# Gated mix of a segment-recurrent attention and a linear-memory attention: float32 partial rows of the output projection, a query pass in column halves, and one attention mask as a matmul

## The chip, the cores and the metric

The kernel runs on one core of a Trainium2 chip. The metric is the device time of one execution in microseconds (us), median of three runs. The engines are called as the profile calls them: PE (TensorE, with PEld for its weight loads), DVE (VectorE), ACT (ScalarE), POOL (GpSimd) and SP (SyncE, which here only issues DMAs, in order, and waits in order).

## The reference

Two attentions read the same 2048 tokens of width 512 and are mixed by a gate per token.

```
# A: 64 segments of 32 tokens, 8 memory tokens carried from one to the next
for s in range(n_seg):
    h = concatenate([mem, x[s*32:(s+1)*32]])          # 40 rows
    q, k, v = h @ Wq, h @ Wk, h @ Wv                  # 32 heads of 128
    p = softmax(where(mask, q k^T * scale, -1e9))     # memory columns open, the rest causal
    o = (p v) @ Wo
    mem = o[:8];  outs.append(o[8:])
# B: 4 blocks of 512 tokens, 32 heads of 16: causal softmax in the block,
#    plus phi(q) M / phi(q) z with M, z summed over the blocks before
g = sigmoid((x * gate_w).sum(-1))
out = g * a + (1 - g) * b
```

The memory of a segment is the first 8 rows of the output of the one before. So the 64 segments of A form one chain, while B and everything that does not depend on the memory can run beside it.

## The kernel before

**How A is cut.** In segment `s` only 32 rows go through the passes that the memory gates: the 8 memory rows and the first 24 tokens. The last 8 tokens of each of four segments (a group, `g = s // 4`, 16 groups) are "left" rows: they need no memory as inputs, and their queries, keys and values are projected together for the group (units `L<g>.…`, `left_units`). The 32 heads lie in two halves, 0 and 1, of 16 heads. Each unit of work has a short name, and `A_ORDER` is a string, written out in full, in which every unit of the whole kernel stands once; `plan_a` walks it, and each unit appends its instructions to the queues of its engines (lines 1678 to 1680). Engines run their queues in order and wait on semaphores; so the string sets the order on each of PE, DVE, ACT, POOL and SP. A `~` behind a name swaps the engine of a copy out of PSUM between ACT and DVE; `A_ENG` has the default.

For segment `s` the units are:

- `K0x K0y K1x K1y Q0x … V1y`: the projections. A pass is for one of K, Q, V and one half of the heads and gives a bank of 512 columns; `x` and `y` are the first and the last two of the four blocks of the contraction (`nat_pass` L1471, `proj` L1248). Each is 8 matmuls, four beside each other in column strips of the array, 512 columns each.
- `k0 k1 q0 q1 v0 v1`: the copies out of PSUM (`nat_ev` L1477). `TK0 TK1 TQ0 TQ1`: transposes on DVE, 128x256 four-byte elements each (`tr` L1486, `flip` L1262).
- `qt`: POOL copies the left queries of the segment beside the others (L1651).
- `S0 S1`: scores on PE (L1498). `X0 X1`: exp on ACT (L1517). `Y0 Y1`: the mask, a `min` with `mkeep` on DVE (L1522; `mkeep` holds 3e38 where a score counts and 0 elsewhere). `M0 M1`: sums on PE by a matmul with ones (L1529). `L0 L1`: reciprocals as ln and exp on ACT (L1543). `N0 N1`: the product on DVE (L1551); `n0 n1`: the product for the left rows on POOL (L1555).
- `PV`: values (L1560), which needs both halves. `E0 … E3`: four copies out (L1586). `W0 … W3`: the product with Wo (L1594, `out_part` L1332): 64 matmuls in all into one bank of 128x256, in which partitions 0 to 63 hold one partial sum (over 16 heads) and 64 to 127 the other.
- `hm`: the recurrence. DVE transposes that bank (L1606), moves half of it (L1607) and adds the two partial sums into the next segment's columns of `xTp` (two instructions, L1611).
- `G` and `H`: the same bank is copied out for the output rows, its two partition halves into `WF[0]` and `WF[1]` (`half_out` L1358, twice 64x256 float32). `ws`: POOL adds them into `WN[s % 2]` in bfloat16 (`sum_rows` L1361), and SP stores that to DRAM as `aTd[s]` (`rows_out` L1365).
- `oL`: POOL keeps the attention output of the left rows in `OTL` (L1632).

For a group: `O<g>.0 … 3` is the product of `OTL` with Wo, `O<g>.e`, `.f` are its two copies, and `.s` the sum on POOL and the store to `aTl[g]` (`ol_units` L1369). `T<g>.l` loads the rows of the group into `aTg` (`load` L1408): four segments, for each a DMA of 24 rows from `aTd` (L1415) and one of 8 rows from `aTl` (L1417), eight in all, six for the last group. `T<g>.b` is B's output projection on PE, and it issues the load of B's next rows; `.t` puts `(1-g)` times it into `t1_sb` on ACT (L1446); `.f` adds `g` times `aTg` on DVE (L1458) and stores the result. The last segment's rows do not go that way: `63.H` finishes them from the bank and stores them by four DMAs.

For B: `bS` (scores of two steps), `bE` (exp on ACT, and for tiles on the diagonal a mask on POOL by `affine_select`, L945), `bP` (values), `bT` (what closes a job), `pj` and `pp` (projections of the last block). B issues its loads as it goes, on SP too, and most of them wait for PE to have read the buffer they fill.

**Before the string** come the loads of x and the weights and B's projections of three blocks; the weights Wk, Wq, Wv of A are loaded in that order.

**Waits.** `_mk_deps` (L88) makes an instruction that writes a tile wait for all readers of it, DMAs included; loads with `scratch=True` wait for the DMAs that stored their rows. DMAs are issued by SP in the string's order.

Of the kernel before, what the change touches and what calls it, by code (L numbers as in the profile page):

```python
# [238 lines left out]
def build(nc, es, A_x, A_mem0, A_Wq, A_Wk, A_Wv, A_Wo, B_wq, B_wk, B_wv, B_wo, B_beta, gate_w, out, dbg=None):  # L239
# [31 lines left out]
    def alloc(stack, *specs):  # L271
        at, spans = 0, {}
        for name, shape, dt, n in specs:
# [15 lines left out]
          ("onesb", [128, 128], BF16, 0), ("mkeep", [128, 224], BF16, 0),  # L289
# [5 lines left out]
          ("WN", [128, 256], BF16, 2), ("tt", [128, 2 * C, SEG], F32, 0), ("tu", [128, 2 * C, M], F32, 0), ("WF", [128, 256], F32, 2), ("OLN", [128, 256], BF16, 0))  # L295
# [17 lines left out]
    v.t1z = v.KTL0[:, :, :, :, :, :].rearrange("p r j k m u -> p (r j k m u)").bitcast(F32)[:, 0:128]  # L313
    v.KTL, v.QTL, v.VL = [v.KTL0, v.KTL1], [v.QTL0, v.QTL1], [v.VL0, v.VL1]
# [3 lines left out]
    def dram(name, shape):  # L318
        t = nc.dram_tensor("scr_" + name, shape, BF16, kind="Internal")
        setattr(v, name, t.ap())  # L320
# [4 lines left out]
    dram("aTd", [NSEG, 64, 256])  # L325
    dram("aTl", [NG, 64, 256])
# [98 lines left out]
def plan_const(v):  # L425
# [29 lines left out]
    def late():  # L455
        rob, rmk = Rs("onesb"), Rs("mkeep")
        gp(lambda g: g.memset(onesb[:], 0.0), rob, "onesb0", True)
# [5 lines left out]
        for j in range(4):  # L463
# [5 lines left out]
            for n in range(2):  # L469
# [5 lines left out]
        v.late_mask = lambda: P.op("dve", lambda d: d.transpose(mkeep[:, :].rearrange("p (i w) -> p i w", w=L + 16)[:, :, L:L + 16], v.mskT[:, :, :, :, :].rearrange("p n (x k) m u -> p (n x) (k m u)", x=2)),  # L475
             reads=[rmt], writes=[rmk], name="mskT")
# [377 lines left out]
class BAttn:  # L854
# [190 lines left out]
    L0.xl 0.K0x L0.QL1x L0.QL0x wl L0.VL0x L0.VL1x wl L0.QL1y L0.VL0y L0.VL1y 0.V0x 0.K0y L0.KL1x L0.VL0e~ L0.KL1y 0.K1x L0.KL0x 0.K1y L0.VL1e L0.KL0y wl  # L1045
    L0.QL0y 0.Q1x L0.KL1e~ 0.Q0x 0.k1~ wl L1.xl 0.k0 L0.KL0e~ L0.QL1e bS L0.QL0e bE 0.TK0 0.Q1y L1.KL0x wl bE bE wl 0.Q0y 0.V1x 0.V1y 0.qt pj 0.q0 0.q1
    0.TQ1 L0.VLt 0.TQ0 0.TK1 pj pj wl 0.S1 0.S0 0.V0y 0.X0 0.Y0 0.X1 pj L1.KL0y 0.Y1 0.v0 0.M1 bE 0.M0 0.L1 L1.KL0e L1.QL0x wl bP L1.QL0y 0.n1 0.L0 0.N1
    0.N0 1.qt 0.v1~ bP 0.n0 0.PV 0.E1 0.E0 0.W0 0.E3~ pp~ 0.E2 bS 0.W1 0.W2 bE 0.W3 bE pj pj bE bE bP bP 0.hm 0.G~ 1.K0x 1.K0y 1.Q0x pp 1.k0~ 1.Q0y 1.K1x
    1.q0~ L1.QL0e~ 1.K1y 1.TK0 1.TQ0 0.H 0.oL 1.Q1x 1.Q1y bS 1.k1 1.V0x pp~ 1.S0 1.q1 bE 1.V0y 1.TK1 1.X0 1.TQ1 1.S1 1.V1x 1.Y0 1.M0 1.v0 bE 1.V1y 1.X1
    1.Y1 bE 1.M1 1.L0 1.v1 pj 1.L1 1.n0 1.N0 pj 1.N1 1.n1 L1.KL1x bE 1.PV 1.E0 1.E1 L1.KL1y bP bP 1.W0 0.ws 1.E2~ 1.W1 1.E3~ 1.W2 pp L1.KL1e~ 1.W3 1.hm bS  # L1050
    1.G~ pj pj bE bE bE 2.qt 2.K1x 2.Q0x 2.Q0y bT 2.K0x 1.H 2.K1y bE 2.q0~ bP 2.K0y bS 2.k1~ pp bP bE bE bE bE 2.k0~ 2.V1x 2.Q1x 2.Q1y 1.ws 2.TK1 2.TQ0
    2.V1y 2.TK0 2.S0 L1.QL1x 2.q1~ 2.TQ1 2.V0x 2.S1 pj 2.X0 2.Y0 1.oL 2.M0 2.v1~ pj 2.X1 2.L0 2.Y1 2.M1 2.V0y bP pj 2.n0 2.N0 pp~ bP 2.L1 pj 2.v0~ 2.N1 pj
    2.n1 2.PV pj 2.E0~ L1.QL1y pp 2.E2 2.E1 2.E3~ L1.QL1e~ 2.W0 2.W1 2.W2 2.W3 bS 3.qt pp~ bE 2.hm bE bE L1.VL0x L1.VL0y 3.K1x 2.G~ 3.K0x L1.VL0e bE 3.K0y
    3.Q1x 3.k0 3.Q1y bT bP 2.H 3.K1y bS 3.TK0 3.q1 3.k1 bP 3.TQ1 3.Q0x 3.Q0y 3.V1x bE 3.TK1 3.q0 3.S1 bE 3.V1y 3.TQ0 pj 3.S0 3.V0x bE 3.X1 3.Y1 3.v1 bE
    3.X0 3.M1 3.L1 pj 3.Y0 3.M0 3.L0 bP 2.oL 2.ws 3.n0 3.n1 bP pp~ 3.N1 bS 3.V0y bE pj pj 3.N0 3.v0 bE bT 3.PV bE L1.VL1x pp 3.E0 4.qt 3.E1 L1.VL1y 3.W0
    3.E2~ 3.E3 3.W1 bE bP bP 3.W2 3.W3 bS L1.VL1e~ bE pj bE 3.hm bT pj 4.K1x 3.oL 4.Q1x bE 4.K1y 4.K0x 4.Q1y pp bE 4.q1 4.k1~ 4.K0y 4.k0 4.Q0x 4.Q0y 4.TK1
# [12 lines left out]
    bE L3.KL1y bE bE L3.QL0x 9.Q1x 9.Q1y 9.K1x 9.K0x bE 9.q1~ L3.KL1e~ 9.K0y 9.K1y 9.Q0x 9.Q0y 9.TQ1 9.V1x 8.G~ 9.k0 bP 9.k1 9.TK1 9.S1 9.TK0 9.V1y 9.q0~
    9.TQ0 9.S0 9.X1 9.V0x 9.Y1 9.X0 10.qt 9.M1 9.v1 9.Y0 9.V0y 9.L1 9.M0 9.v0 O1.0 9.L0 bP 9.n1 8.H 9.N1 9.n0 8.ws 9.N0 O1.1 bT 9.PV 9.E0 9.E1~ 9.E2~ 9.E3  # L1070
    L3.QL0y 9.W0 9.W1 9.W2 9.W3 bS 9.oL bE bT 9.hm O1.2 bE L3.QL0e~ O1.3 10.K0x bE bT 10.K0y 10.Q0x 10.Q0y bE 10.K1x O1.e~ 10.k0 10.Q1x 10.Q1y 10.q0~
    10.TQ0 10.q1 10.TK0 10.K1y O1.f~ 10.TQ1 10.V0x 10.k1 T0.l 10.S0 10.X0 10.TK1 10.V0y 10.v0~ O1.s 10.V1x 10.Y0 10.S1 10.X1 10.M0 10.Y1 10.L0 10.V1y
    L3.QL1x 10.v1 10.M1 bP L3.VL0x 10.L1 bP 10.n0 9.G 10.n1 L3.VL0y 10.N0 10.N1 10.PV 9.H L3.VL0e~ 10.E0 9.ws 10.E1~ L3.QL1y 10.E2~ 10.E3~ 10.W0 10.W1
    L3.QL1e~ 10.W2 10.W3 bS bE 10.hm T0.b 11.K1x 11.Q1x 10.G 11.K1y 10.H 11.k1~ 11.Q1y 11.TK1 11.qt T0.t bE bE 11.q1 11.TQ1 T0.f 10.ws 11.K0x 11.K0y bE
    11.Q0x 11.Q0y 11.k0 bP bP 10.oL 11.TK0 11.S1 bS 11.q0~ 11.V1x 11.TQ0 11.X1 11.S0 11.Y1 bE 11.X0 11.M1 11.V1y 11.L1 11.n1 11.V0x 11.Y0 11.v1 11.M0
    11.N1 11.V0y L3.VL1x bE 11.L0 11.n0 L3.VL1y 11.v0 11.N0 bE 11.PV bE 11.E3~ bP bP 11.E0~ 11.E1~ 11.W0 11.E2 11.W1 11.W2 12.qt L3.VL1e~ L3.VLt L4.xl
    11.W3 bT bS bE bE 11.oL 11.hm bT 11.G bE 12.K1x 12.K1y bE 12.k1 12.Q1x 11.H 12.Q1y 12.K0x 12.TK1 12.Q0x 12.Q0y 12.K0y 12.q1 12.TQ1 bP 12.S1 bP bS
    12.q0 12.k0 12.V0x 12.TQ0 12.X1 12.TK0 12.S0 12.V0y bE bE 12.Y1 12.X0 12.M1 12.V1x 12.Y0 12.M0 12.V1y L4.KL0x 12.L1 12.L0 L4.KL0y 12.v0 12.N1 12.v1~
    12.N0 12.n1 12.n0 12.PV bE L4.KL1x 12.E0 12.E1~ 12.W0 12.E2 11.ws 12.E3 12.W1 12.W2 12.W3 12.hm L4.KL1y O2.0 O2.1 13.Q0x 13.K1x 13.K1y L4.KL0e~ 13.qt
    L4.KL1e 13.Q1x 13.Q1y 13.k1~ 13.K0x 12.G 13.Q0y 12.oL 13.q1 T1.l 13.q0~ 13.K0y 12.H~ 13.TQ1 13.TK1 O2.2 13.S1 13.k0 13.X1 13.TQ0 13.TK0 bE 13.Y1  # L1080
# [144 lines left out]
def plan_a(v, nseg):  # L1225
# [237 lines left out]
    def segment(s):  # L1463
# [149 lines left out]
        def w_ev(i=1):  # L1613
# [9 lines left out]
            if i:  # L1623
                B.give(wb["bk"])
# [90 lines left out]
```

## Time and profile before

| | us |
|---|---|
| runs | 862.77, 863.67, 869.02 |
| median | 863.67 |
| the profiled execution, its own time | 861.26 |
| its span, first to last instruction | 859.5 |
| start of the first transpose of the recurrence (L1606) | 76.28 |
| start of the last one (63 in all) | 842.09 |

| engine | busy us | share of the span | instructions |
|---|---|---|---|
| PE | 794.1 | 92% | 22005 |
| PEld | 445.9 | 52% | 22011 |
| DVE | 615.5 | 72% | 1525 |
| ACT | 572.8 | 67% | 1326 |
| POOL | 322.8 | 38% | 790 |

The granted TensorE clock was 0.995 on average. Busy time of PE counts a matmul until it has passed the array, while the next one already runs; so PE's busy share is not the share of its peak. The transposes of L1606 mark where one segment ends and the next begins; the distance between two of them is called the length of a segment below. The DMA engines are nearly full in the first 60 us, while the weights come in, and mostly idle behind that.

### The profile page before, as it was taken

To read this page: it belongs to the slowest core of one execution; us is meant where nothing else is said; L and a number is where in the kernel's file an instruction comes from. 1 tells how busy PE (TensorE), PEld (TensorE's weight loads), DVE (VectorE), ACT (ScalarE), POOL (GpSimd) and SP (SyncE) were. 2 spreads that over 40 slices of the span, in tenths; PEclk is the share of its full clock that TensorE was granted. 3 is DMA by queue.
4 is the path that set the end of the run, shared out by engine and by line. 5 is a ranking of instruction groups with operands and counts; after the bars stand their busy time and mean duration, and the time that the engine had idled before them with its cause. 6 is when DMAs were issued, how large, how long until landed. Compare 5 with 4: busy or idle time off the path is not lost.

```text
span 859.5 us, 49189 instructions
## 1 busy us (share of the span) xinstructions
PE 794.1 (92%) x22005; PEld 445.9 (52%) x22011; DVE 615.5 (72%) x1525; ACT 572.8 (67%) x1326; POOL 322.8 (38%) x790
## 2 busy tenths in 40 slices
PE   8979999999998999999999999999899998999786
PEld 4534555555555555555555455555454555545354
DVE  4536677686678876788677887778667777788455
ACT  5536687868677577776756767775477675785543
POOL 4503344443324344353324434342233343453222
PEclk9999999999999999999999999999999999999999
DMA  9995421112202110111211111111202111020211
GB/s 330 415 371 153 101 69 54 24 51 47 49 23 51 28 47 23 41 35 38 43 24 52 27 51 24 39 32 43 49 11 57 28 42 33 21 55 5 64 29 32
DMA packets 103631, 58.23 MB, mean 68 GB/s; under 512 B 74196, under 2 KB 97532, under 8 KB 101884
## 3 DMA queue, kind: packets, MB, share of 16 engines
q1 hardware_dynamic: 102700, 54.29, 21.9%
q8 instruction: 172, 2.82, 1.3%
q10 hardware_dynamic: 720, 0.80, 0.3%
q14 instruction: 39, 0.32, 0.1%
HBM read 37.23 MB, written 17.82 MB: 64 GB/s over the span
## 4 chain that ended last, share of the span: by engine, by line
PE 58%; DVE 13%; ACT 11%; DMA 7%; POOL 4%; issue 4%; SPq 3%; ACTq 0%; POOLq 0%; DVEq 0%
PE ps L1255 32%; PE ps L1342 13%; POOL PT L945 2%; ACT PT L939 2%; PE ps L1569 2%; DVE tt L1606 2%; DVE xTp L1611 2%; DVE V_sb L376 2%; PE ps L918 2%; ACT R_sb L1548 2%; PE ps L971 2%; DMA Wv_sb<-in_A_Wv_dram 2%; DVE P_sb L1552 2%; DMA scr_kqd<-stgk 2%; PE ps L1505 1%
## 5 line engine op out<-in xcount | busy, mean ns | idle before, releaser
L939 ACT ACTIVATE PT<-ps 128x512 bf16<-128x512 f32 x320 | 174.7, 600 | 64.6 <-PE ps L918 46.8
L945 POOL TENSOR_SCALAR_AFFINE_SELECT PT<-PT 128x128 bf16<-128x128 bf16 (+2 forms) x320 | 120.1, 375 | 217.9 <-ACT PT L939 197.7
L1255 PE MATMUL ps<-Wv_sb,xTp 128*32 128x512 bf16 x2048 | 145.3, 379 | 0.1
L1255 PE MATMUL ps<-Wq_sb,xTp 128*32 128x512 bf16 x2048 | 137.0, 380 | 5.4 <-DVE xTp L1611 3.8
L1255 PE MATMUL ps<-Wk_sb,xTp 128*32 128x512 bf16 x2048 | 137.1, 380 | 4.3 <-DVE xTp L1611 3.4
L1342 PE MATMUL ps<-Wo_sb,OT_sb 128*32 128x256 bf16 x4032 | 123.7, 275 | 3.7 <-ACT OT_sb L374 3.0
L1342 PEld LDWEIGHTS ps<-Wo_sb,OT_sb 128*32 128x32 bf16 x4032 | 102.9, 97 | 27.3 <-ACT OT_sb L374 23.7
L374 ACT ACTIVATE OT_sb<-ps 128x320 bf16<-128x320 f32 x169 | 64.0, 439 | 38.3 <-PE ps L1580 37.6
L1557 POOL TENSOR_TENSOR P_sb<-P_sb,R_sb 128x64 bf16<-128x64 bf16 x128 | 46.5, 364 | 113.7 <-ACT R_sb L1548 111.2
L1255 PEld LDWEIGHTS ps<-Wq_sb,xTp 128*32 128x32 bf16 x2048 | 55.3, 97 | 63.1 <-DVE xTp L1611 13.0
L1255 PEld LDWEIGHTS ps<-Wk_sb,xTp 128*32 128x32 bf16 x2048 | 55.6, 97 | 61.2 <-DVE xTp L1611 8.9
L374 ACT ACTIVATE KN_sb<-ps 128x512 bf16<-128x512 f32 x93 | 55.6, 600 | 45.8 <-PE ps L1255 45.6
L374 ACT ACTIVATE QN_sb<-ps 128x512 bf16<-128x512 f32 x91 | 54.2, 599 | 44.0 <-PE ps L1255 43.4
L376 DVE CAST V_sb<-ps 128x512 bf16<-128x512 f32 x101 | 69.3, 687 | 6.9 <-PE ps L1255 5.9
L1606 DVE STREAM_TRANSPOSE tt<-ps 128x256 f32<-128x256 f32 x63 | 28.3, 449 | 50.8 <-PE ps L1342 50.0
L1267 DVE STREAM_TRANSPOSE KT_sb<-KN_sb 128x256 f32<-128x256 f32 x128 | 54.8, 431 | 12.3 <-ACT KN_sb L374 9.8
L1267 DVE STREAM_TRANSPOSE QT_sb<-QN_sb 128x256 f32<-128x256 f32 x128 | 54.0, 429 | 9.5 <-ACT QN_sb L374 7.4
L376 DVE CAST OT_sb<-ps 128x320 bf16<-128x320 f32 x87 | 40.0, 485 | 29.1 <-PE ps L1580 28.6
L1519 ACT ACTIVATE P_sb<-ps 128x224 bf16<-128x224 f32 x128 | 45.7, 359 | 21.7 <-PE ps L1510 14.6
L1363 POOL TENSOR_TENSOR WN<-WF 64x256 bf16<-64x256 f32 x63 | 46.0, 730 | 26.7 <-ACT WF L374 14.4
L1523 DVE TENSOR_TENSOR P_sb<-P_sb,mkeep 128x224 bf16<-128x224 bf16 x128 | 37.3, 292 | 25.1 <-ACT P_sb L1519 23.2
L1255 PEld LDWEIGHTS ps<-Wv_sb,xTp 128*32 128x32 bf16 x2048 | 43.2, 95 | 18.1 <-issue 1.9
(138 smaller groups left out, 1383.7 us busy)
## 6 DMA issues: line engine op xcount, KB each, us to landing
Wk_sb<-in_A_Wk_dram SPq DMA_DIRECT2D x4, 1024.0 KB, 10.5
Wq_sb<-in_A_Wq_dram SPq DMA_DIRECT2D x4, 1024.0 KB, 14.0
Wv_sb<-in_A_Wv_dram SPq DMA_DIRECT2D x4, 1024.0 KB, 15.8
Wo_sb<-in_A_Wo_dram SPq DMA_DIRECT2D x8, 512.0 KB, 6.2
scr_vld<-VNL SPq DMA_DIRECT2D x16, 256.0 KB, 2.2
VL<-scr_vld SPq DMA_DIRECT2D x64, 64.0 KB
scr_kqd<-stgk SPq DMA_DIRECT2D x12, 256.0 KB, 10.0
Vj<-scr_vd SPq DMA_DIRECT2D x32, 68.0 KB, 2.4
```

The lines of the kernel that those rows point to most:

```text
L374: P.op("act", lambda a: a.activation(dst, src, ACT.Copy), reads=[v.rbank[k] for k in bks], writes=dres, name=name)
L376: P.op("dve", lambda d: d.tensor_copy(dst, src), reads=[v.rbank[k] for k in bks], writes=dres, name=name)
L939: P.op("act", lambda a: a.activation(pt, v.pb[bk], ACT.Exp, scale=v.SCALE_B), reads=[v.rbank[bk]], writes=[rp], name="be%d_%d" % (n, t))
L945: P.op("gp", lambda g: g.affine_select(mv, mv, [[0, len(cut)], [1, 128]], ALU.is_ge, 0.0, base=0, channel_multiplier=-1), reads=[rp], writ ...
L1255: ins = pe.matmul(pb[bk][SEG * j:SEG * (j + 1), :], lhs(c), cols(w, j) if split else w[:, 512 * j:512 * (j + 1)], start=(c == 0), stop=(c ...
L1267: P.op("dve", lambda d: d.transpose(to, src), reads=reads, writes=writes, name=name)
L1342: ins = pe.matmul(pb[bk][SEG * j:SEG * (j + 1), 0:256], lhs(h), Wo_sb[:, h, :].rearrange("p (k q c) -> p q k c", q=2, c=64)[:, j % 2], sta ...
L1363: P.op("gp", lambda gq: gq.tensor_tensor(dst[0:64, :], v.WF[0][0:64, :], v.WF[1][0:64, :], ALU.add), reads=[Rs("WF0"), Rs("WF1")], writes= ...
L1519: P.op("act", lambda a: a.activation(P_sb[:, b, :], pb[bk][:, 0:So], ACT.Exp, scale=SCALE), reads=[rbank[bk]], writes=[Rs("Pm%d" % b), Rs( ...
L1523: P.op(ENG["y"], lambda d: d.tensor_tensor(P_sb[:, b, :], P_sb[:, b, :], mkeep[:, :], ALU.min), reads=[Rs("mkeep")], writes=[Rs("Pm%d" % b ...
L1557: P.op(ENG["n"], lambda d: d.tensor_tensor(left, left, grp04(R_sb[:, b, :]), ALU.mult), reads=[Rs("R0_%d" % b)], writes=[Rs("PL%d" % b)], ...
L1606: P.op("dve", lambda d: d.transpose(v.tt[:, :, :].rearrange("p (k n) t -> p k n t", n=2), src), reads=[rbank[wb["bk"]]], writes=[Rs("tt")] ...
```

## The change

Four things are changed together.

1. **Float32 partial rows.** The bank of Wo's partial sums is copied out once, whole, into a float32 tile `WN` of 128x256 (unit `H`; `G` is gone), of which there is one, shared by the segments and by the groups' `O<g>.e`. POOL no longer adds there; SP stores all 128 rows in float32 (`aTd`, `aTl` are 128x256 float32). `T<g>.l` loads the two partial sums into two float32 tiles, `aF` and `t1_sb`, eight DMAs each (six for the last group); a new unit `T<g>.a` adds them on POOL, 128x512 float32; `.t` then overwrites `t1_sb`, and `.f` reads `aF`.
2. **Q1 in column halves.** `Q1x` and `Q1y` are now each a bank of 256 columns over all four blocks of the contraction (16 matmuls of 256 columns each); `q1x`, `q1y` copy 128x256 out, and `TQ1x`, `TQ1y` transpose 128x128 four-byte elements.
3. **The mask of half 1 as a matmul.** `Z1` writes `mbias` (0 or -1048576) into the score bank by four matmuls with a 128x32 piece of the identity, 224 columns each; `S1` then accumulates onto it, and `Y1` is gone. `Y0` stays. `mbias` is made once, by one DVE instruction.
4. **A new order string**, 4509 units in place of 4444, with other engines for some copies (`~`).

```diff
-          ("WN", [128, 256], BF16, 2), ..., ("WF", [128, 256], F32, 2), ("OLN", [128, 256], BF16, 0))
+          ("WN", [128, 256], F32, 0), ..., ("aF", [128, DM], F32, 0))
...
-    dram("aTd", [NSEG, 64, 256])
-    dram("aTl", [NG, 64, 256])
+    dram("aTd", [NSEG, 128, 256], F32)
+    dram("aTl", [NG, 128, 256], F32)
...
+            P.op("dve", lambda d: d.tensor_scalar(v.mbias[:, :], mkeep[:, :], 1048576.0, -1048576.0, op0=ALU.min, op1=ALU.add), ..., name="mbias")
...
         def u2():
-            half_out(st["bk"], 0, ENG["O0"], "olev%d_0" % g)
+            evac(ENG["O0"], v.WN[:, :], pb[st["bk"]][:, 0:256], [st["bk"]], [Rs("WN")], "olev%d" % g)
+            B.give(st["bk"])
         def u3():
-            half_out(st["bk"], 1, ENG["O1"], "olev%d_1" % g)
-            B.give(st["bk"])
-        def u4():
-            sum_rows(v.OLN, Rs("OLN"), "ols%d" % g)
-            rows_out(v.aTl[g], v.OLN[0:64, :], ...)
+            rows_out(v.aTl[g], v.WN[:, :], [Rs("WN")], ...)
...
-            for r in range(3 if last else 4):
-                P.dma(grp, ... rows[SEG * r:SEG * (r + 1) - M], v.aTd[4 * g + r].rearrange("(q t) (k c) -> t k q c", q=2, c=64)[M:SEG] ...)
-                P.dma(grp, ... v.aTl[g].rearrange("(q r i) (k c) -> r i k q c", q=2, r=4, c=64)[r] ...)
+            for i, (t, res) in enumerate(((v.aF, "aF"), (t1_sb, "t1_"))):
+                for r in range(3 if last else 4):
+                    P.dma(grp, ... v.aTd[4 * g + r].rearrange("(h q t) (k c) -> h t k q c", h=2, q=2, c=64)[i, M:SEG] ...)
+                    P.dma(grp, ... v.aTl[g].rearrange("(h q r i) (k c) -> r h i k q c", h=2, q=2, r=4, c=64)[r, i] ...)
+        def ua():
+            P.op("gp", lambda gq: gq.tensor_tensor(v.aF[0:top], v.aF[0:top], t1_sb[0:top, :], ALU.add), reads=[Rs("t1_")], writes=[Rs("aF")], name="asum%d" % g)
...
-            P.op("dve", ... scalar_tensor_tensor(fin[0:top], fin[0:top], g_sb[0:top, g:g + 1], t1_sb[0:top, :], ALU.mult, ALU.add) ...)
+            P.op("dve", ... scalar_tensor_tensor(fin[0:top], v.aF[0:top], g_sb[0:top, g:g + 1], t1_sb[0:top, :], ALU.mult, ALU.add) ...)
...
+        def half_pass(m, b, half):
+                for c in range(C):
+                    for j in range(4):
+                        ins = pe.matmul(pb[bk][SEG * j:SEG * (j + 1), 0:256], lhs(c), cols(w_sb[:, c, 2048 * b + 1024 * half:2048 * b + 1024 * (half + 1)], j), start=(c == 0), stop=(c == C - 1))
...
+        def bias(b):
+                for j in range(4):
+                    ins = pe.matmul(pb[bk][SEG * j:SEG * (j + 1), 0:So], v.id32[:, :], v.mbias[:, :], start=True, stop=False, skip_group_check=True)
...
         def scores(b):
-                        ins = pe.matmul(..., start=True, stop=True, skip_group_check=True)
+                        ins = pe.matmul(..., start=new, stop=True, skip_group_check=True)
...
-        def w_ev(i=1):
+        def w_ev():
-                half_out(wb["bk"], i, ENG["H%d" % i], "wev%d_%d" % (s, i))
+                evac(ENG["H0"], WN[:, :], pb[wb["bk"]][:, 0:256], [wb["bk"]], [rw], "wev%d" % s)
...
         def w_rows():
-            sum_rows(WN, rw, "wsm%d" % s)
-            rows_out(v.aTd[s], WN[0:64, :], ...)
+            rows_out(v.aTd[s], WN[:, :], ...)
```

Of the order, one segment before and after (group units and B's units stand between):

```
before  47.Q0x 47.Q0y 47.Q1x 47.K1x 47.K1y 47.Q1y 47.q0~ 47.K0x 47.k1 47.TK1 47.K0y 47.q1 47.TQ1 47.S1 47.V0x 47.k0 47.TQ0 47.TK0 47.X1 47.Y1 47.S0 47.V1x 47.X0 47.M1 47.V1y 47.L1 47.Y0 47.v1 47.M0 47.n1 47.L0 47.n0 47.N1 47.N0 47.V0y 47.v0~ 47.PV
after   46.E2 47.Z1 46.W0 46.W1 46.W2 46.E3~ 46.W3 46.hm 46.H 47.Q0x 47.K0x 47.Q0y 47.K0y 47.K1x 47.k0 47.K1y 47.k1 47.q0 47.Q1x 47.q1x 47.Q1y 47.TQ0 47.TK0 47.S0 47.q1y 47.X0 47.TK1 47.TQ1x 47.V0x 47.TQ1y 47.V0y 47.S1 47.Y0 47.M0 47.X1 47.L0 47.V1x 47.M1 47.V1y 46.ws 47.v0 47.n0 47.N0 47.L1 47.v1~ 47.N1 47.n1 47.PV
```

and two places around the groups' loads after:

```
12.oL O2.1 13.N1 13.PV L4.QL1e~ T1.l L4.QL0y 13.E0 bP 13.E1 13.E3~ 14.Z1 13.W0 13.W1 12.ws 13.E2 14.qt 13.W2 L4.QL0e~ 13.W3 bS bE O2.2 bE O2.3 13.hm O2.e~
63.q0 63.K0y O15.s 63.k1~ T14.t 63.q1x 63.V0x T14.f T15.l 63.TK1 ... 63.PV 63.E0 T15.a 63.W0 63.E1~ 63.W1 63.E2 63.E3 T15.t 63.W2 63.W3 63.H T15.f
```

More of the change, by code (lines that the diff above doesn't have):

```diff
@@ L1496, in segment, with f_bias @@
         So = 4 * LW
+        def bias(b):
+            bk = sbk[b] = B.take()
+            def f_bias(pe):
+                ins = None
+                for j in range(4):
+                    rows = slice(SEG * j, SEG * (j + 1))
+                    ins = pe.matmul(pb[bk][rows, 0:So], v.id32[:, :], v.mbias[:, :], start=True, stop=False, skip_group_check=True)
+                return ins
+            P.op("pe", f_bias, reads=[Rs("id32"), Rs("mbias")], writes=[rbank[bk]], name="msb%d_%d" % (s, b))
         def scores(b):
-            bk = sbk[b] = B.take()
+            new = b not in sbk
+            if new:
+                sbk[b] = B.take()
+            bk = sbk[b]
             def f_sc(pe):
@@ L1505, in f_sc @@
                         ins = pe.matmul(pb[bk][SEG * j:SEG * (j + 1), LW * i:LW * i + L], head(KT_sb, 16 * b + 4 * j + i),
[L1506 removed]
+                                        head(QT_sb, 16 * b + 4 * j + i), start=new, stop=True, skip_group_check=True)
                 for k in range(2):
@@ L1643, in segment @@
                 units["T%s%d" % (m, b)] = lambda m=m, b=b: tr(m, b)
-            for u, fn in (("S", scores), ("X", expo), ("Y", mask), ("M", sums), ("L", recip), ("N", norm), ("n", norm_left)):
+            for u, fn in (("Z", bias), ("S", scores), ("X", expo), ("Y", mask), ("M", sums), ("L", recip), ("N", norm), ("n", norm_left)):
                 units["%s%d" % (u, b)] = lambda b=b, fn=fn: fn(b)
```

449 lines of the change are left out of this document (239 added, 210 removed).

## The prediction

> **What bounds the kernel now.** I read the page first, then PE's waits, then the 62 lengths between the transposes of L1606, then the timeline of one segment, and at the end the groups and SP's part of the timeline.
>
> ```profile
> PE 794.1 (92%) x22005; PEld 445.9 (52%) x22011; DVE 615.5 (72%) x1525; ACT 572.8 (67%) x1326; POOL 322.8 (38%) x790
> ```
> ```profile
> PE ps L1569 <- DVE P_sb L1552: 9.6, 30, 1.5
> PE ps L1255 <- DVE xTp L1611: 7.2, 22, 0.6
> PE ps L971 <- POOL PT L945: 5.6, 11, 0.9
> PE ps L1580 <- DMA VL<-scr_vld: 3.2, 3, 1.5
> PE ps L1255 <- DMA Wv_sb<-in_A_Wv_dram: 3.1, 1, 3.1
> ```
>
> PE looks full, and its two commonest waits are for half 1's product (L1552) and for the memory (L1611): one chain closes every segment. The lengths show it. They sum to 842.1 - 76.3 = 765.8 us, 12.35 each; but 26 of 62 lie between 11.55 and 11.89 us whatever PE has to do in them (segment 31 has no unit of B's attention, segment 38 has two bS and four bP). Counting units by their rows (a half pass 0.432 us for 8 matmuls, a score 0.165, sums 0.105, PV 0.40, a quarter of Wo 0.465, of `O` 0.455, bS 0.35, bP 0.125, `T.b` 0.864), PE has 9.3 to 13.9 us of work in a segment, 10.75 in the mean. So about 11.6 us is a floor set by latency. Segment 31 in the timeline, its chain alone:
>
> ```profile
> 448.18 0.45 DVE L1606 STREAM_TRANSPOSE tt<-ps 128x256 f32<-128x256 f32 x1 [0.55 <-PE ps L1342]
> 449.33 0.61 PE L1255 MATMUL ps<-Wq_sb,xTp 128*32 128x512 bf16 x8
> ...
> 453.08 0.59 ACT L374 ACTIVATE KN_sb<-ps 128x512 bf16<-128x512 f32 x1
> ...
> 453.70 0.45 DVE L1267 STREAM_TRANSPOSE KT_sb<-KN_sb 128x256 f32<-128x256 f32 x1
> ...
> 454.66 0.36 ACT L1519 ACTIVATE P_sb<-ps 128x224 bf16<-128x224 f32 x1 [0.25 <-PE ps L1538]
> ...
> 455.05 0.28 DVE L1523 TENSOR_TENSOR P_sb<-P_sb,mkeep 128x224 bf16<-128x224 bf16 x1
> ...
> 455.38 0.28 PE L1538 MATMUL ps<-P_sb,onesb 128*32 128x160 bf16 x8
> ...
> 456.82 0.38 PE L1569 MATMUL ps<-P_sb,V_sb 32*128 32x40 bf16 x32 [0.27 <-DVE P_sb L1552]
> ...
> 459.84 0.45 DVE L1606 STREAM_TRANSPOSE tt<-ps 128x256 f32<-128x256 f32 x1 [0.19 <-PE ps L1342]
> ```
>
> The reader is to see: passes, then a 512-column copy (0.59), a transpose (0.45), scores, exp (0.36), mask (0.28), sums, and so on to the next transpose 11.66 us later. If each segment took the larger of 11.6 and its PE work plus 0.3 (the fullest, segment 26, took 11.68 with 11.36 of work), the 62 would take 728.2; the other 37.6 us are single waits. SP is the part that the page hardly shows:
>
> ```profile
> 802.74 0.67 SPq L1417 DMA_DIRECT2D aTg<-scr_aTl  x1
> 803.45 0.77 SPq L1415 DMA_DIRECT2D aTg<-scr_aTd  x1
> 808.24 0.75 DVE L1458 SCALAR_TENSOR_TENSOR aTg<-aTg,g_sb,t_sb 128x512 bf16<-128x512 bf16 x1 [4.17 <-DMA aTg<-scr_aTl]
> 810.41 0.28 PE L1505 MATMUL ps<-QT_sb,KT_sb 128*32 128x40 bf16 x16 [2.22 <-DVE QT_sb L1267]
> ```
>
> A load of a group's rows holds SP 0.67 or 0.77 us, eight of them 6.2 to 7.0. Here they came late, DVE waited 4.17 us, and segment 60 took 15.15.
>
> **Half 1's chain, the main term.** Removed: the mask; exp ends at 455.02, sums start at 455.38, and without it they would follow at about 455.07, so -0.31. The last copy is 256 columns, not 512: ACT's 64x256 row has 377 ns, its 320-column row 439; I take 385 in place of 590, -0.21. The transpose is 128 columns: 431 ns for 256 and 708 for 512 (L995) give 0.29, with the 128-column row of L1273, 409 ns, as the dear end; -0.14. Against it: exp of half 1 would now fall on half 0's ln and exp (0.30 + 0.34) on ACT, for which I give back 0.15. The floor becomes 11.1, between 10.9 (no collision) and 11.6 (half 0, whose mask and whole copies stay, or ACT takes its place).
>
> **PE's added work.** `Z1`: the sums' 160 + 64 columns take 0.10 us (four matmuls each), so 224 columns by four take the same: 6.4 us for 64. Q1's halves: Wo's 64 matmuls of 256 columns took 1.86 us, 0.116 for four, so 0.93 for 32 against 0.864 for 16 of 512: 4 us. Where `Z1` stands between the values and the first Wo product, as 47.Z1 does, it lies under PE's wait for the copies; elsewhere it is full price. PE's work per segment, counted in the new string, becomes 10.87. The larger of floor and work plus 0.3, summed over 62 segments, is 706.6 at a floor of 10.9, 712 at 11.1, 722.6 at 11.4 and 730.8 at 11.6. I take 712 with the same 37.6 of waits: **-16 us**, ends -21.6 and +2.6.
>
> **Copies and sums.** 79 pairs of copies of 64x256 (ACT 377, DVE 415 ns) become 79 copies of 128x256; DVE loses 64 masks (18.7 us) and gains some 10 in half transposes; POOL loses 46.0 + 11.8 us of sums and gains 16 sums of 128x512 float32 at about 1.4 (twice the 730 to 750 ns of 256 columns). None of the three was the bound, so I price this at nothing: between -3 (PE's 5.6 us of waits for POOL's L945 partly go) and +2 (more on ACT). `mbias` and its 128x32 piece of the identity are two short instructions ahead of the string, under the loads.
>
> **Start.** PE waited 3.14 us for Wv and then ran 3.41 us at half clock, some 1.7 lost. The new string puts Wq and Wk passes, one bS and two `pj` ahead of the first Wv pass, about 3 us of work: **-4**, ends -6 and 0.
>
> **SP's queue, the main cost.** Each group loads 16 times, 8 x 0.77 + 8 x 0.69 = 11.7 us on SP, 13.1 until landed (some 1.4 more), against 6.2 before. Behind them in the queue stand the stores of `ws`, loads of `VL` and B's loads. And two things now wait on SP that did not: POOL's sum `T.a`, with `n`, `qt` and B's masks queued behind it; and the copies `H` and `O.e`, for `WN` is one tile and its next writer waits until the store has landed, on ACT or DVE, ahead of copies that the chain needs. I walked SP's queue through both strings: each DMA starts when the one before ends, its data are there and its buffer is read, with units placed by their PE work. For the string before this gives the start of 15 of the 16 load groups within 3.5 us of the trace. For the new one, at some 12.2 us a segment, POOL waits at `T.a` in 12 of 16 groups, 1.4 to 4.7 us in the middle (T2.a 3.1, with 17.qt 2.3 us behind it; T12.a 4.7, with 60.n1 2.0 behind it), and `WN` is waited for eight times, 0.9 to 4.2 us, some 19 in all (33.H 3.3, O11.e 2.3, O12.e 3.0, O14.e 4.2). Bounds: 0, where all of it lies in idle time or SP runs ahead (T1.l and T10.l can start 7 to 11 us early), and +27, where `WN`'s 19 and the 8 of T2.a and T12.a reach PE whole. The nearest row, segment 60, lost 2.2 us of PE for 4.2 on DVE, one group in sixteen; most of the new waits are shorter, and on engines with slack. I take **+4**, nearer to that row than to the far end.
>
> **The clock after a wait.** After a wait of 1.49 us for `VL` at 613.4, PE ran 3.41 us at half clock: 64 matmuls of Wo took 3.37 us where they take 1.93. After the 2.22 us at 808 it did not. [...]
>
> **End.** `T15.l` is 12 loads, 8.8 us on SP against 4.4, and waits for `T14.f`, which now waits for `T14.a` and 16 loads; then come a sum (1.4), t1 (0.69), the last addition (0.76) and a store. Before, that addition waited 1.72 us and still came ahead of the last product. **+3**, ends 0 and +8.
>
> **Sum.** The profiled execution took 861.3 (span 859.5, 1.8 around it). 861.3 - 16 - 4 + 4 + 3 = 848.3. The median of the runs, 863.7, stands 2.4 above it, so 850.7; I say **850**.
>
> **Rivals.**
> *SP's queue decides.* The loads reach POOL and `WN`'s writers late and the chain with them: 861.3 - 16 - 4 + 27 + 8 + 2.4 = 879, slower. For it: SP's rows, and T14.a stands 3 us behind T14.l. Against it: SP is in use only 385 of 860 us. It decides from waits that cost PE over 23 us (4 + 3 are counted). Chance 0.25.
> *The floor stays.* Half 0, or ACT with two ln and exp pairs, ends as late as half 1 did; the floor is 11.4: 861.3 - 5.7 - 4 + 4 + 3 + 2.4 = 861, no change. For it: in segment 31 half 0's product ended at 456.17, only 0.6 ahead of half 1's. Against it: half 0's passes now always come first. Chance 0.17.
> *More.* Floor 10.9 and no SP wait reaches PE: 861.3 - 21.6 - 6 + 2.4 = 836. Chance 0.08.
> The forecast has 0.50, with its own range 840 to 858.
>
> **How the numbers follow.** About 1% is what a measurement of this kernel can tell from no change, so faster is below 855.0 and slower above 872.3. Faster: 0.45 of the forecast, 0.08 of *more*, 0.02 of the floor: 0.55. Same: 0.05 + 0.14 + 0.02 = 0.21. Slower: 0.24. The range, 834 to 878, reaches from *more* to just under the first rival's time and leaves out about 0.15.
>
> **What would show it.** Right: lengths of 11.1 to 11.3 in segments without B's work; `xTp` and the `P_sb` product still PE's commonest waits; no wait for Wv. SP's rival: DVE and ACT copies into `WN` that wait for a DMA, POOL's sum waiting for `aF` or `t1_sb` loads 2 us and more, scores waiting for `qt`. The floor rival: lengths still at 11.5, with ACT's ln and exp end to end. I am wrong if a load of 256-byte float32 runs holds SP less than the 0.7 us of the rows, or if the new lengths scatter without a floor.

## The result, and the profile after

The changed kernel took 893.6 us (median of 4 runs, 891.1 to 896.4), beside 863.8 for the kernel before: a ratio of 1.033, 95% interval 1.028 to 1.039. It is slower by 30 us; forecast were 850, with 879 for the rival "SP's queue decides". The profiled execution took 896.4, its span is 893.3. Cut at the same marks as before, the first transpose of the recurrence (now L1653) and the last:

| | before | after | forecast |
|---|---|---|---|
| until the first transpose | 76.3 | 80.5 | -4 |
| the 62 lengths | 765.8 | 784.9 | -16 + 4 |
| behind the last transpose | 17.4 | 27.9 | +3 |

The page of the changed kernel, its engines' line and, by engines, the chain of work that ended last:

```profile
PE 805.2 (90%) x23291; PEld 497.2 (56%) x23291; DVE 575.8 (64%) x1459; ACT 572.2 (64%) x1378; POOL 291.5 (33%) x728
PE 56%; SPq 18%; DMA 7%; issue 6%; DVE 5%; ACT 5%; POOL 3%; POOLq 0%; DVEq 0%; ACTq 0%
```

The chain of the kernel before:

```profile
PE 58%; DVE 13%; ACT 11%; DMA 7%; POOL 4%; issue 4%; SPq 3%; ACTq 0%; POOLq 0%; DVEq 0%
```

DVE and POOL are less busy, as the change intends, and the time did not fall with it. SP's queue was on 3% of the chain before and is now on 18%. PE's waits (us, times, longest) show why:

```profile
PE ps L1268 <- ACT WN L375: 7.6, 4, 3.6
PE ps L1616 <- DVE P_sb L1599: 5.4, 8, 1.7
...
PE ps L924 <- DMA QTj<-scr_kqd: 4.2, 1, 4.2
...
PE ps L1585 <- ACT P_sb L1566: 3.6, 1, 3.6
```

The two waits that led this list before, for half 1's product (9.6 us, 30 times) and for the memory (7.2, 22 times), have shrunk: the first to 5.4 in 8. The chain of a segment did get shorter: the shortest lengths are 11.2 to 11.4 where they were 11.55 to 11.65. In place of many short waits stand a few long ones, and at the root of most are copies into `WN` (the 3.6 us for `P_sb` too: ACT's exp stood behind such a copy at 542). The view of that tile says what its writers waited for (us, times), and the view of `aF` what a load costs SP (ns: shortest, median, longest) and what POOL's sum waited for:

```profile
  DMA scr_aTd<-WN: 30.5, 8
...
  DMA scr_aTl<-WN: 13.4, 4
```
```profile
L1419 SPq DMA_DIRECT2D aF<-scr_aTd x63: 767/768/1719, 200.0 to 878.6; - x63
L1421 SPq DMA_DIRECT2D aF<-scr_aTl x63: 662/662/1065, 200.9 to 879.4; - x63
...
  DMA t_sb<-scr_aTl: 35.8, 5
  issue: 25.1, 7
```

The load's price is what the prediction took from the rows before (0.77 and 0.67), and a group holds SP for 12.2 to 13.4 us. But twelve copies waited 43.9 us, not eight 19, and POOL's sums 60.9 (in 25.1 of them, called issue, the view names no releaser). One case in the timeline, the loads of group 8 from the end of segment 43 on:

```profile
617.72 0.38 ACT L375 ACTIVATE WN<-ps 128x256 f32<-128x256 f32 x1
617.93 0.77 SPq L1419 DMA_DIRECT2D t_sb<-scr_aTd  x1
...
623.84 0.66 SPq L1421 DMA_DIRECT2D t_sb<-scr_aTl  x1
...
624.54 0.45 SPq L1373 DMA_DIRECT2D scr_aTl<-WN  x1
...
627.42 0.38 ACT L375 ACTIVATE WN<-ps 128x256 f32<-128x256 f32 x1 [7.17 <-DMA scr_aTl<-WN]
...
627.86 1.90 PE L1268 MATMUL ps<-Wk_sb,xTp 128*32 128x512 bf16 x16 [3.61 <-ACT WN L375]
```

The left tokens' sums are copied into `WN` at 617.7. Their store stands in SP's queue behind the loads that began at 611.7 and goes out at 624.5. The next copy, segment 43's own, needs the same tile; ACT, with all its other copies queued behind, stands still for 7.2 us, and PE, which wants the bank, for 3.6. Then the granted clock drops. In the windows of the profile it is the last number but two, 1.00 from 616 to 624 and 0.59 from 628.0 to 631.4:

```profile
616.00:624.00 8.00, 7.88 (x220) 4.53 (x212) 3.42 (x11) 3.61 (x11) 1.67 (x4) 1.00 0.20 44
...
628.00:631.40 3.40, 3.40 (x56) 1.87 (x52) 1.21 (x3) 2.00 (x5) 0.00 (x0) 0.59 0.37 96
```

Over the whole run, PE lay idle for 61.7 us behind the first 77 (waits of over 0.3 us; 33.1 before), and 37.3 us ran at half clock (0.50 granted) behind the first 30 (8.7 before), with PE busy in 25.7 of them (6.8). Half of PE's busy time there, 12.8 us (3.4), is my estimate of what the clock took.

### The profile page after: what moved, and what is told of

Its sections match the earlier page's. It is cut to its first block, busy times and chain, and to the rows that moved or that the text cites. A ratio compares the mean times of both kernels' runs of the same rounds, so it can differ in the third digit from the quotient of the medians.

```text
span 893.3 us, 51818 instructions
## 1 busy us (share of the span) xinstructions
PE 805.2 (90%) x23291; PEld 497.2 (56%) x23291; DVE 575.8 (64%) x1459; ACT 572.2 (64%) x1378; POOL 291.5 (33%) x728
## 4 chain that ended last, share of the span: by engine, by line
PE 56%; SPq 18%; DMA 7%; issue 6%; DVE 5%; ACT 5%; POOL 3%; POOLq 0%; DVEq 0%; ACTq 0%
PE ps L1268 27%; PE ps L1355 10%; SPq L1419 8%; SPq L1421 6%; PE ps L1492 4%; PE ps L1616 2%; PE ps L924 2%; PE ps L977 2%; POOL PT L951 2%; DMA scr_kqd<-stgk 1%; DMA scr_aTd<-WN 1%; ACT PT L945 1%; SPq L892 1%; PE ps L1552 1%; DMA QTj<-scr_kqd 1%
## 5 line engine op out<-in xcount | busy, mean ns | idle before, releaser
L951 POOL TENSOR_SCALAR_AFFINE_SELECT PT<-PT 128x128 bf16<-128x128 bf16 (+2 forms) x320 | 122.9, 384 | 221.7 <-ACT PT L945 202.5
L1268 PEld LDWEIGHTS ps<-Wk_sb,xTp 128*32 128x32 bf16 x2048 | 59.3, 97 | 59.6 <-ACT WN L375 8.3
L375 ACT ACTIVATE QN_sb<-ps 128x256 bf16<-128x256 f32 (+1 forms) x149 | 65.1, 441 | 36.5 <-PE ps L1268 24.4
L1492 PE MATMUL ps<-Wq_sb,xTp 128*32 128x256 bf16 x2048 | 74.7, 276 | 5.0 <-ACT WN L375 2.3
L1268 PE MATMUL ps<-Wq_sb,xTp 128*32 128x512 bf16 x1024 | 71.4, 380 | 1.8 <-ACT PT L945 1.2
L1280 DVE STREAM_TRANSPOSE QT_sb<-QN_sb 128x128 f32<-128x128 f32 (+1 forms) x192 | 62.8, 335 | 11.9 <-ACT QN_sb L375 9.8
L377 DVE CAST V_sb<-ps 128x512 bf16<-128x512 f32 x78 | 53.4, 687 | 23.9 <-PE ps L1268 22.7
L1653 DVE STREAM_TRANSPOSE tt<-ps 128x256 f32<-128x256 f32 x63 | 28.3, 449 | 55.6 <-PE ps L1355 55.4
L1599 DVE TENSOR_TENSOR P_sb<-P_sb,R_sb 128x160 bf16<-128x160 bf16 x128 | 43.2, 347 | 21.6 <-ACT R_sb L1595 20.5
L377 DVE CAST OT_sb<-ps 128x320 bf16<-128x320 f32 x81 | 37.2, 484 | 29.3 <-PE ps L1627 29.3
L375 ACT ACTIVATE WN<-ps 128x256 f32<-128x256 f32 x54 | 20.9, 387 | 52.7 <-DVE tt L1653 24.0
```

The source lines that it names most:

```text
L375: P.op("act", lambda a: a.activation(dst, src, ACT.Copy), reads=[v.rbank[k] for k in bks], writes=dres, name=name)
L377: P.op("dve", lambda d: d.tensor_copy(dst, src), reads=[v.rbank[k] for k in bks], writes=dres, name=name)
L951: P.op("gp", lambda g: g.affine_select(mv, mv, [[0, len(cut)], [1, 128]], ALU.is_ge, 0.0, base=0, channel_multiplier=-1), reads=[rp], writ ...
L1268: ins = pe.matmul(pb[bk][SEG * j:SEG * (j + 1), :], lhs(c), cols(w, j) if split else w[:, 512 * j:512 * (j + 1)], start=(c == 0), stop=(c ...
L1280: P.op("dve", lambda d: d.transpose(to, src), reads=reads, writes=writes, name=name)
L1492: ins = pe.matmul(pb[bk][SEG * j:SEG * (j + 1), 0:256], lhs(c), cols(w_sb[:, c, 2048 * b + 1024 * half:2048 * b + 1024 * (half + 1)], j), ...
```

## The experiments

Each is compared with the kernel before, run beside it (medians 861.8 to 863.3). SP's queue was the suspect; the rivals were the rest of the change (matmuls and order) and the single tile.

**1. Quick loads (eight_loads).**

```diff
-    rows = t[:, :].rearrange("p (k q c) -> p k q c", q=2, c=64)          # two tiles, two loops
-    ... v.aTd[4 * g + r].rearrange("(h q t) (k c) -> h t k q c", h=2, q=2, c=64)[i, M:SEG]
+    rows = v.aF2[:, :, :].rearrange("p i (q n) -> p (i q) n", q=2)       # one tile, one loop
+    ... v.aTd[4 * g + r].rearrange("(a t) n -> t a n", a=4)[M:SEG]
```

> The changed kernel (893.6), but the two halves of a group's rows lie side by side in one tile and keep the order that the partial sums are stored in, so that one transfer brings both: 8 loads on SP per group in place of 16, in pieces of 1 KB in place of 256 B; the last sum is made in two instructions on DVE. Theory 'queue' (16 loads hold SP for 12.2 to 13.4 us per group, and all that lies behind them in SP's queue is late): a group takes 5.5 to 6.5 us as in the kernel before (6.2), and the time falls to 858 to 868. Rival 'work and order' (the column halves, the mask on TensorE and the new order carry the loss): 885 to 894. Rival 'one tile' (that the copies of Wo's sums have one tile for all): SP is held half as long, so about half the loss goes, 872 to 884.

Measured: **849.8**, 0.987 of before (0.984 to 0.989). That is 44 us off the changed kernel, faster than the kernel before, and below the 858 to 868 that "queue" expected. That it is also the time that had been forecast is luck (the end of the next section). A load is now 0.3 us in the median, and a group holds SP for 2.9 to 4.6 us; two copies are left that wait for a store (the view of `WN`):

```profile
L1419 SPq DMA_DIRECT2D aF<-scr_aTd x63: 290/299/1553, 197.2 to 834.3; - x63
L1421 SPq DMA_DIRECT2D aF<-scr_aTl x63: 263/308/1322, 197.8 to 834.6; - x63
```
```profile
  DMA scr_aTd<-WN: 7.9, 2
```
```profile
PE 793.7 (94%) x23291; PEld 495.5 (59%) x23291; DVE 580.1 (69%) x1475; ACT 570.2 (67%) x1378; POOL 286.9 (34%) x728
PE 76%; DVE 7%; ACT 6%; DMA 4%; issue 3%; POOL 2%; SPq 1%; ACTq 0%; POOLq 0%; DVEq 0%
```

PE is on 76% of the chain, where it was on 58% before the change. Matmuls, halves, mask and order are those of the changed kernel, so "work and order" falls.

**2. Sixteen loads in the quick shape (sixteen_q).**

```diff
-    ... rearrange("(a t) n -> t a n", a=4)[M:SEG]
+    for h in range(2):   w = slice(2 * h, 2 * h + 2)
+        ... rearrange("(a t) n -> t a n", a=4)[M:SEG, w]
```

> As eight_loads (849.8), but each half by a load of its own: 16 loads per group again, in the 1 KB pieces of eight_loads (two per partition and load). Theory 'shape' (what a load costs SP is set by the pieces of its access pattern: 334 to 420 ns in eight_loads, 665 to 806 ns in the changed kernel): 16 loads at 0.33 to 0.42 hold SP for 5.3 to 6.7 us per group, as the 8 loads of the kernel before did (6.2), and the time comes to 851 to 862. Rival 'number' (a load costs SP what it costs, whatever its pieces): 10 us or more per group, 870 to 890.

Measured: 852.1, 0.986 (0.982 to 0.991). Sixteen loads of such a shape hold SP for 5.7 to 8.0 us, 6.5 in the mean, about as eight did before the change. It is the shape, not the number:

```profile
L1421 SPq DMA_DIRECT2D aF<-scr_aTd x126: 291/297/1600, 198.8 to 838.6; - x126
L1423 SPq DMA_DIRECT2D aF<-scr_aTl x126: 264/303/1562, 199.5 to 838.9; - x126
```

So 3.4 us of SP per group (the mean of eight_loads) gives 849.8, 6.5 gives 852.1 and 12.2 or more gives 893.6: the first 3 us more cost 2, within the scatter of the runs, and the next 6 cost 41. I read this as an edge, where SP's stretch no longer ends before the next store is wanted; no run places it between 6.5 and 12.2.

**3. Own tiles for the copies (wn_own).**

```diff
+    def wn(n, s):      # from segment 20 on: columns of x that are no longer read
+        return (v.WN, Rs("WN")) if s < 20 else (xTp[:, n, 0:512].bitcast(F32), Rs("WX%d" % n))
-    WN, rw = v.WN, Rs("WN")
+    WN, rw = wn(s % 2, s)            # the left tokens' sums: wn(2, ...)
```

> The changed kernel (893.6), but from segment 20 on the copies of Wo's sums have three tiles in place of one (two by turns for segments, one for the left tokens), in columns of x that no one reads any more; loads and queue as they are. Of the 12 waits of a copy for a store (43.9 us), 10 are in these segments. 'One tile': the loss goes but for what is before segment 20 and at the ends, 866 to 874. 'Queue': the copies no longer wait, but POOL's sum (61 us of waiting), the loads of the other attention and the stores do, 878 to 888. 'Work and order': within 3 us of 893.6.

Measured: 873.9, 1.015 (1.009 to 1.020): 20 of the 44 come back though SP is held as long. That is the upper end of what "one tile" expected; one wait for a store is left (3.2 us, in segment 11). In the changed kernel 11 of the 12 waits, not 10, lie from segment 20 on. The rest of the loss could be POOL's sum or what else stands in the queue.

**4. POOL's sum later (sum_late).** On top of wn_own, the string alone: `T<g>.a`, with `.t` and `.f` behind it, moved to about 1.35 segments behind `T<g>.l`.

> As wn_own (873.9: the changed kernel, 16 slow loads per group, copies in three tiles from segment 20 on), and POOL's sum, with the scaling and the gate that follow it, is moved later in the order, to about 1.35 segments (16 us) behind its group's first load in place of 0.2 to 1.1, for the 12 groups where there is room; so POOL should find the loads landed. Theory 'two waits' (SP's 12 us do harm where a copy and where POOL's sum wait for them, and nowhere else): what wn_own left of the loss goes, 852 to 862. Rival 'all of SP's queue' (the other attention's loads and the stores behind the 12 us matter as much): 866 to 874.

Measured: 881.1, 1.021 (1.017 to 1.025), slower than without the move (873.9) and above both ranges expected. POOL's wait fell (DMA 20.3 and issue 3.6, from 26.8 and 21.8), but I had put ACT's scaling right behind the sum, and it took the wait over:

```profile
ACT t_sb L1459 <- POOL aF L1431: 23.3, 9, 5.5
```

So this tells nothing of the two theories; a wait was moved from an engine with slack to one without.

**5. and 6. SP held, but the rows in time (hold_shared, hold_own).**

```diff
     ... the 8 loads of eight_loads
+    for each of 12 (source rows as in the changed kernel):
+        P.dma(..., lambda sp: sp.dma_start(v.dup[g, n, ...].rearrange("t (k q c) -> t k q c", q=2, c=64), src), ...)
```

> As eight_loads (849.8), but behind its 8 loads each group issues 12 more on SP, in the 256 B pieces of the changed kernel, from the stored rows into a scratch tensor that no one reads: SP is held some 12 us per group again, and the group's own rows land as early as in eight_loads. POOL's sum has nothing to wait for; the one tile for the copies stays. Theory 'the tile' (of the 44 that lie between eight_loads and the changed kernel the larger part is copies that wait for a store behind the 12 us): 868 to 880. Rival 'POOL's sum' (the rows that land late are the cause, and SP's queue itself is harmless): 850 to 856.

> As hold_shared, with the copies in three tiles from segment 20 on. Theory 'the tile': no one waits for the late stores, and 850 to 857 is left. Rival 'all of SP's queue' (the other attention's K, Q and V loads behind the 12 us are waited for by TensorE): 860 to 872.

Measured: 887.0 (1.031; 1.024 to 1.038) with the one tile, 860.5 (0.997; 0.994 to 0.999) with own tiles. With the one tile the copies wait as in the changed kernel, and with own tiles they do so once, before segment 20 (the views of `WN`, first hold_shared, then hold_own):

```profile
  DMA scr_aTd<-WN: 32.9, 9
...
  DMA scr_aTl<-WN: 10.0, 4
```
```profile
  DMA scr_aTd<-WN: 4.9, 1
```

Both came out above what "the tile" expected (868 to 880, 850 to 857), and hold_own lies at the lower end of the rival's range, "all of SP's queue". The 44 us, taken apart in this order, by differences of medians:

| step | us | PE idle | lost to half clock (that estimate) |
|---|---|---|---|
| eight_loads | 849.8 | 27.9 | 3.1 |
| + SP held 12 us, nobody waits for the tile from segment 20 on (hold_own) | +10.7 | 33.9 | 7.8 |
| + one tile for all copies (hold_shared) | +26.5 | 54.6 | 11.4 |
| + the rows themselves late, for POOL (changed kernel) | +6.6 | 61.7 | 12.8 |

"The tile" is the largest part, and hold_own's 10.7 hold one wait of that kind too, in segment 11, which is 18.0 us long where eight_loads has 12.0. "POOL's sum" as the main cause falls. The shares depend on the order of the steps: with the rows late, own tiles are worth 19.7 (changed kernel against wn_own), not 26.5, and with own tiles late rows cost 13.4 (wn_own against hold_own), not 6.6. The 6.6 alone is within the scatter of the runs (885.6 to 897.5 against 891.1 to 896.4). What is left to the other transfers is 10.7 at most; in hold_own's PE waits the loads of `VL` come to 3.5 us. The idle and lost columns explain it: from eight_loads to the changed kernel 33.8 more idle and 9.7 more lost, 43.5 of a difference of 46.5 in the spans.

**7. and 8. Two parts of the chain undone, on top of quick loads (eight_y1, eight_whole).** `Z1` left out of the string and `Y1` put behind `X1`; `SPLIT = ()` with `Q1x Q1y q1 TQ1` as whole units.

> As eight_loads (849.8), but the mask of half 1 is the minimum on DVE again, right behind that half's exponentials, and TensorE's four matmuls for it are left out of the order. Theory 'chain' (a segment is as long as its chain from projection to memory rows): 0.28 of the shortest DVE masks come back per segment, up to 62 x 0.28 = 17, where the other half isn't the later one: 856 to 868. Rival 'TensorE' (a segment is as long as its matmuls): 6.4 us of matmuls go, 843 to 850.

> As eight_loads (849.8), but half 1 of the query is projected, copied and transposed whole (one copy of 512 columns and one transpose, each put where the second of the two halves stood). Theory 'chain': the last copy takes 0.60 in place of 0.44 and the last transpose 0.43 in place of 0.33, so 0.26 per segment, 62 x 0.26 = 16 where this half is the later one: 855 to 868. Rival 'TensorE': 2048 matmuls of 256 columns (73.5 us) become 1024 of 512 (71.5): 846 to 850.

Measured: 872.8 without the mask on TensorE (1.011; 1.006 to 1.017), 857.9 without the halves (0.995; 0.992 to 0.997). So in this order they are worth 23 and 8 us, the first more than the 17 that "chain" had at most; "TensorE" falls for both: with 256 and 1024 matmuls fewer the time went up. The shortest lengths: 11.20 in eight_loads, 11.35 and 11.49 in these two, 11.55 before.

**9. The mask alone in the old order (z_in_before).** `Y1` out, `Z1` right ahead of `S1`, in the string of before.

> The kernel before (863.8), in its own order, but the mask of half 1 is the four matmuls on TensorE, set right ahead of that half's scores, and the minimum on DVE goes (one tile in place of two for the rows' sum before segment 20, for room). Theory 'chain': half 1's chain loses a DVE instruction of 0.28 and gains 0.1 on TensorE per segment: 62 x 0.15 to 0.28, 846 to 855. Rival 'fit' (in an order that was written for the mask on DVE half 1 comes first in most segments, and half 0's chain is the longer then): 860 to 871.

Measured: 862.3, 1.000 (0.998 to 1.003), as "fit" expected. This kernel has one tile in place of two for the rows' sum before segment 20, and nothing in that tile's view waits for a store. The same edit is worth 23 us in the new string and nothing in the old one. The shortest lengths stay at 11.56. So experiments 7 and 8 measure a part together with an order written around it, not the part.

**10. The rows alone in the old order (rows_in_before, rows8_in_before).** First with the changed kernel's loads; in four groups (3, 6, 9, 10) the string puts POOL's sum ahead of its loads, so it adds what the tiles still hold, and the rows of these groups are wrong. Then with quick loads, stores kept behind their copies, and `T<g>.a .t` some 0.45 segments behind `T<g>.l`.

> The kernel before (863.8) with its order, its masks and its whole query pass, but Wo's sums as float32 rows of both halves, one tile for the copies, 16 loads per group and one sum per group on POOL (set ahead of the scaling of the other attention's rows). 'Queue': SP is held some 12 us per group here too, 885 to 900. 'Work and order': the copies and sums saved pay for the loads, 858 to 868. 'One tile': as 'queue'.

> The kernel before (863.8) with its masks and its whole query pass, but Wo's sums as float32 rows, brought in by the 8 loads per group of eight_loads; stores follow their copies before the one tile is written again, and each group's sum on POOL stands ahead of the scaling of the other attention's rows, some 0.45 segments behind its loads. Theory 'rows cost nothing once SP is held 3 us per group' (63 copies and sums of half the partitions go, the chain stays): 858 to 866. Rival 'fit' (ACT's scaling now waits for POOL's sum, in an order not written for that): 868 to 885.

Measured: 991.8 (1.150; 1.147 to 1.153) and 890.4 (1.031; 1.025 to 1.037). Both beyond what was expected. With quick loads SP's hold is short (2.8 to 4.9 us per group); here the waits that show are for the new dependences, the tile (its writers wait for stores) and ACT's scaling for POOL's sum. No run splits the 28 us between them:

```profile
  DMA scr_aTd<-WN: 18.7, 11
  DMA scr_aTl<-WN: 5.7, 5
```
```profile
ACT aF L1436 <- POOL aF L1408: 29.2, 13, 5.6
```

**11. The old rows in the new order (old_rows).** Two half copies `G` and `H`, the sum on POOL at `ws`, eight bfloat16 loads, in the changed kernel's string with `G` set ahead of `H`.

> The changed kernel with its order, column halves and mask on TensorE, but Wo's sums go as in the kernel before: two copies of half the partitions, a sum on POOL per segment, bfloat16 rows, 8 loads per group (the second copy stands beside the first in the order). 'Queue': the loss of the rows is gone and the shorter chain stays, 848 to 862. 'Work and order': 882 to 894. 'One tile': as 'queue'.

Measured: 908.0, 1.053 (1.050 to 1.056): both theories missed. Two copies from one bank on two engines wait for each other there (`_mk_deps` makes readers of a bank on different engines follow each other), and the next passes wait for the bank:

```profile
PE ps L1268 <- ACT WF L375: 19.5, 16, 2.9
```

**12. A later first score, and own tiles, with quick loads (eight_start).** `bS` and its `bE` set behind ten projection units in place of five, `wn` as in experiment 3.

> As eight_loads (849.8), with the copies of Wo's sums in three tiles from segment 20 on (as in wn_own), and the first scores of the other attention set behind ten projection units in place of five, so that their query load (waited for 4.2 us) lands under matmuls. Expected: the start piece falls from 79.3 to 75 to 77, the last piece from 21.1 to 17 to 18 (the copy's wait of 3.8 us for a store goes), the other such wait (4.0 in segment 53) goes: 838 to 844. Rival 'transfers bound the start' (the 16 engines are busy throughout until 60 us): the start stays at 79, 843 to 847.

Measured: 849.2, 0.983 (0.979 to 0.987). The wait for `QTj` fell from 4.2 to 1.4 us, but the start stayed at 79.1: a wait of 1.56 for `VL` came, and a second stretch at half clock (granted 0.83 in the mean from 70 to 80 us, 1.00 there in eight_loads). The rival was right on the start. Own tiles bring nothing once SP is held for 3 us: the two waits, 7.9 us together, went and the end piece fell from 21.1 to 20.3 only.

## Why the prediction was wrong

- **SP's queue, the step that failed.** Taken at +4, bounded at +27; it cost 893.6 - 849.8 = **44**. The parts were right: 16 loads at 0.77 and 0.69 (measured 0.77 and 0.66 in the median), 12 us per group, POOL waiting in 12 of 16 groups, `WN` waited for. Three things were wrong. The walk found 8 waits of 19 us in all where there were 12 of 43.9. The value was taken near one row of the kernel before (4.2 us on DVE, 2.2 on PE), a late group load; no copy of Wo's sums waits for a store there, so that row did not price such waits, and hold_shared against hold_own shows 26.5 for them. And the far end counted a wait once, without the clock. The rival "SP's queue decides" had this mechanism and, with 879, was still 15 us short.
- **The clock after a wait.** The prediction had a row for it (3.37 us for 64 matmuls that take 1.93) and no term in the sum. In the changed kernel PE was busy for 25.7 us at half clock, before for 6.8; by the estimate of half, 12.8 lost against 3.4, so about 9.
- **Half 1's chain, -16: right in size.** With SP held as long as before (sixteen_q), the 62 lengths sum to 748.9, against 765.8: -16.9. The shortest length moved from 11.55 to 11.2; forecast was a floor from 11.6 to 11.1. That the gain comes from the mask and the halves alone is not shown: undone one at a time they cost 23 and 8, more than 16.9 together, and experiment 9 says the mask does nothing without the new order. So the right size may be luck.
- **PE's added work, some 10 us under the floor:** no run measures its size. Leaving out `Z1` or the halves made nothing faster.
- **Copies and sums, 0:** nothing contradicts that the busy time saved is worth nothing, but no run has it alone. The cost is in the waits that took the place of the sums.
- **Start, -4: wrong sign.** 79.3 in eight_loads, +3.1. The wait for Wv went, and one of 4.2 for `QTj` came. The start also took in work of the segments: the matmuls of the left rows' K and Q there rose from 96 to 128, and PE's busy time from 66.7 to 69.2 us. The experiment that shortened the wait moved the time to the next one.
- **End, +3:** +3.7 with quick loads; +10.5 in the changed kernel, where SP's 12 us and a wait of 6.3 for the tile fall into it.

With the measured +3.1, -19.5 and +3.7 of eight_loads the sum is -12.7 on the span of 859.5, and its span is 846.8. The forecast's sum was -13, from -4, -12 and +3: the start came out 7 us longer and the lengths 7 shorter than forecast, and the two cancel. That eight_loads takes the forecast's 850 is luck.

## What to carry to other kernels

A DMA queue that is idle for half of the time (SP was in use 464 of 893 us in the changed kernel) can still decide: here its longest stretch without a gap counted (12.2 to 13.4 us), against the time until someone needs what stands behind it, and a buffer with a single copy turned a late store into a stop of the engine that writes it (7.2 us of ACT behind 620). Before adding loads to a queue, look at the shape of their access pattern: laying the rows down in the order in which they were stored made each load two to three times cheaper to issue (299 and 308 ns in place of 768 and 662), and with the number of loads kept (sixteen_q) that turned this change from 3.3% slower to 1.4% faster. In a kernel whose order is written out, a part done alone or undone measures the part and its misfit with the order; a change that leaves the order alone, like the shape of a load, gives a cleaner difference.

## What the runs showed of the hardware

**Issuing a DMA.** From DRAM rows into 24 partitions, a load whose source has four dimensions with runs of 64 float32 held SP for 768 ns in the median (changed kernel, 63 loads each of `aF` and `t_sb`); the same rows with runs of 256 held it for 299 (eight_loads) when it carried both halves (4 runs per partition) and for 297 (sixteen_q) when it carried one (2). The slowest of each took 1719, 1553 and 1600. The kernel before had runs of 64 bfloat16 in the same four dimensions, half the bytes, and 768 too. The same source into DRAM rows (hold_shared) held SP for 609. Dimensions and length of a run change together here; no run separates them.

**The granted clock and PE's idle time.** The changed kernel's stretches at half clock (0.50 granted) begin at 53.94 us and then 120, 143, 168, 234, 240 and 243 times 3.413 us later; each lasts 3.413 us or twice that, but for the last, which runs on past the span. In the kernel before they begin at 55.49 us and 164 and 235 times 3.413 us later. I cut these two traces into pieces of that length and summed PE's idle time (matmuls and weight loads) in each piece that ran at full clock, as long as PE still had work. All 7 pieces with 2.23 us idle or more were followed by half clock, none of those with 1.72 or less; of the 5 between, those with 1.74 (before) and 1.82 (changed kernel) were, and those with 1.76, 1.79 and 1.93 (changed kernel) were not. So in these traces the idle time alone does not decide between 1.74 and 1.93. The prediction's two rows are among the pieces: the one with the wait of 1.49 us held 1.74 us of idle time and was followed by half clock; of the wait of 2.22 us 1.64 fell into one piece, and nothing followed. The 1.82 are two shorter waits in one piece, 0.57 us and the end of one of 1.70 (behind 879.5). By an estimate from 3.413 us at 0.50, such a stretch takes 1.7 us of matmul time where PE is busy throughout; in the prediction's row it took 1.44 (3.37 - 1.93).
